# Forgetting attention and a bilinear feed-forward on one core: reciprocals for two query blocks at once, constants made by GpSimd, and a new order of all engines

## The chip, the cores and the metric

The kernel runs on one core of a Trainium2 chip. Its engines are TensorE (PE in the profile), VectorE (DVE), ScalarE (ACT), GpSimd (POOL) and SyncE (SP), which here only issues DMAs. Each engine takes its instructions in the order in which the program lists them, and waits on semaphores for what others make. The metric is the device time of one launch in microseconds. Three runs of the kernel before gave 401.5, 402.34 and 403.08 us.

## The reference

Eight batches of eight heads with 576 positions and 64 dimensions go through causal attention with forget gates; its output, as 4608 tokens of 512 values, goes through a feed-forward of width 1536 in which two projections are multiplied. Inputs and output are float32.

```python
scores = scale * np.matmul(q, k.transpose(0, 1, 3, 2))          # scale = 1/8
cum = np.cumsum(np.log(np.clip(f, 0.0001, 1.0)), axis=-1)
decay = cum[:, :, :, None] - cum[:, :, None, :]
scores = np.where(causal, -1000000000.0, scores + decay)
scores = scores - np.max(scores, axis=-1, keepdims=True)
attn = np.exp(scores)
attn = attn / (np.sum(attn, axis=-1, keepdims=True) + 1e-09)
x = np.matmul(attn, v).transpose(0, 2, 1, 3).reshape(B * S, H * D)
out = ((x @ w_a) * (x @ w_b)) @ w_out
```

## The kernel before

**Work.** A tile t stands for two heads of a batch, so there are 32 tiles; a unit is two tiles (four heads of a batch), 16 in all. A tile's 576 queries are five blocks: blocks 0 to 3 have 128 rows and block i has i + 1 key blocks up to the diagonal; block 4 has the last 64 rows of both heads, one above the other on the partitions. TensorE makes the scores of a unit in four groups of blocks (L401; `groups = [(1, 0), (2,), (3,), (4,)]`, taken in the turn 0, 1, 3, 2), with 32 rows of q and k at a time. Batches 0 to 2 add the decay with matmuls too and VectorE takes the row maxima (L488); for the others VectorE adds decay and takes the maximum in one instruction (L512). ScalarE takes the exponential and the row sum (L544, L550), one instruction for each head and block, except block 4, where one does both heads. VectorE takes the reciprocals of the sums (L557 for block 4, one column; L559 for the others, two columns, one for each head), and GpSimd multiplies the rows by them (L567, the norms). Tiles of probabilities are called PA (blocks 0 to 2) and PB (blocks 3 and 4); some lie in memory called spread or S. They are transposed, for batch 0 by TensorE into PSUM (psP, L591, copied out by VectorE or ScalarE), for the others by a DMA that SyncE issues (L583), into PTA, PTB and, early, xT. TensorE multiplies them by v (pv, L611, L613, L623 and, for block 4, L636), and ScalarE or VectorE copies the result to xT, the transposed tokens.

**Feed-forward.** For 256 to 512 tokens, TensorE makes psa and psb (L874) for each of twelve blocks of the width; psa is cast to a (L138 on ScalarE, L142 on VectorE), VectorE multiplies it by psb (L890), and TensorE makes the output pso (L899), which is copied to osb and stored (L914). The weights come by seven DMAs that GpSimd issues (L365) and that cast to 16 bits: 512 columns of wa and wb, then the other 1024 of each, then wout in three parts. The first psa and psb can run once batch 0 is through its attention and the first two loads are there.

**Start.** The forget gates f are clipped (L206), their logarithm is summed along the row (L213) and kept in a high and a low half (L142, L220) in 16 bits, which TensorE spreads over the rows (`rows`, L225). q and k are cast (L140, L142) and transposed in blocks of 32 by VectorE (L302). Constants (ones, a lower triangle `low`, `pick`, `eye`, `neg`, `sel`) come from the identity matrix.

**What sets the order.** All this is put into a list of numbered operations with what each depends on. A table written into the kernel, ORDER, lists the numbers in the order in which they are issued, for all engines together; a second, CHOICE, has a letter for each operation that more than one engine may do. The scheduler follows both as they stand (`tc.manual_schedule()`). Forty of the operations are fillers: four matmuls on the identity (L178, tile `idle`) with no use but to keep TensorE busy. PSUM has four banks for small tiles (tag ff: psa, psb, pso, pv, psP, idle, rows) and two double ones for scores (tag sc).

Of the kernel before, what the change touches and what calls it, by code (L numbers as in the profile page):

```python
# [14 lines left out]
MUL = mybir.AluOpType.mult  # L15
# [22 lines left out]
def kernel(  # L38
# [38 lines left out]
    def fixed(name, shape, dt=FP16):  # L77
        return perm.tile(shape, dt, tag=name, name=name)
# [5 lines left out]
    pick = fixed("pick", [128, 16])  # L84
    warm = fixed("warm", [128, 1], FP32)
# [62 lines left out]

    def lows(_):
        nc.vector.memset(low, 0.0)  # L150
        for a in range(1, 4):
            nc.vector.memset(low[:, a, 0:32 * a], 1.0)
        nc.vector.tensor_tensor_scan(out=step, data0=cw["1"][:, 0:32], data1=eye, initial=0.0, op0=MUL, op1=ADD)
        diag = spare[0][:, 1536:2176].rearrange("p (a x) -> p a x", x=160)[:, :, 0:32]
        nc.vector.tensor_scalar(out=diag, in0=step.unsqueeze(1).to_broadcast([128, 4, 32]), scalar1=-1.0, scalar2=1.0,
                                op0=MUL, op1=ADD)

    def picks(_):
        with nc.allow_low_precision("ones and zeros"):
            nc.vector.tensor_reduce(out=pick, in_=ident.rearrange("p (a r) -> p r a", r=16), axis=AXX, op=ADD)  # L160
            nc.vector.tensor_reduce(out=eye, in_=ident.rearrange("p (a n) -> p n a", n=32), axis=AXX, op=ADD)
        nc.vector.tensor_scalar(out=neg, in0=eye, scalar1=NEGBIG, scalar2=1.0, op0=MUL, op1=MUL)
        nc.vector.memset(sel, 0.0)
        for c in range(SETS):
            for e in range(2):
                nc.vector.tensor_copy(out=sel[:, c, e].rearrange("p (g e r) -> p g e r", e=2, r=16)[:, :, e],
                                      in_=eye[0:32, 16 * c:16 * c + 16].unsqueeze(1).to_broadcast([32, 4, 16]))
# [13 lines left out]
    o_pick = op("D", "pick", picks, [o_id])  # L181
# [15 lines left out]
    def f_ones(_):  # L197
        nc.vector.memset(warm, 1.0)
        nc.vector.memset(cw["1"], 1.0)
# [36 lines left out]
    o0 = op("D", "ones", f_ones)  # L236
# [3 lines left out]
    for lo, hi in ((0, 256), (256, S)):  # L240
# [7 lines left out]
        for n in range(SETS):  # L248
            bm = op("E", "crep", lambda _, n=n, a=a: rows_mm(n, *a), [o4, o5, o_pick], hi - lo)
# [5 lines left out]
    o_low = op("D", "low", lows, [o0, o_pick])  # L255
# [298 lines left out]
    def do_recip(t, i):  # L554
        st = T[("st", t)]
        if i == 4:
            nc.vector.reciprocal(out=st[:, 28:29], in_=st[:, 18:19])  # L557
        else:
            nc.vector.reciprocal(out=st[:, 20 + 2 * i:22 + 2 * i], in_=st[:, 10 + 2 * i:12 + 2 * i])  # L559
# [87 lines left out]

    last_row = [[] for _ in range(RING["bc"])]
# [16 lines left out]
    def softmax(t, g, qk, sc, rows, st_users, pu, norms):  # L665
# [4 lines left out]
        for i in groups[g]:  # L670
# [49 lines left out]
            rc = op("D", "rec", lambda _, i=i: do_recip(t, i), es)  # L720
            st_users[t].extend(es + [rc])
            for h in range(1 if i == 4 else 2):
                nm = op("P", f"norm{i}", lambda e, i=i, h=h: do_norm(e, t, i, h), [rc])
                st_users[t].append(nm)
                pu[kp].append(nm)
                norms.setdefault((t, part), []).append((i, nm))
# [252 lines left out]
    for t0, n in [(0, 256), (256, 256), (512, 256), (768, 384)] + [(1152 + 512 * n, 512 if n < 6 else 384) for n in range(7)]:  # L979
# [3 lines left out]
        42-44 0 20 41 2 1 64 26 31 23 54 55 45 16 32 13 12 71 46 37 47 56 18 67 27 65 34 72 73 68 48 24 19  # L983
# [3 lines left out]
        142 6 154 155 92 147 143 159 149 91 148 144 160 162 161 108 166-168 145 172 131 52 53 132 179 173 14  # L987
# [4 lines left out]
        310 305 1610 1612 246 214 247 158 226 215 227 311 234 189 1611 235 157 222 449 1614-1616 1613 283  # L992
        312 340 195 294 1617 223 1618 1620 228 229 341 1619 347 1621 236 342 450 94 343 191 232 288 1622 349
        260 237 233 1623 242 348 282 300 1624 366 211 344 1625 240 261 243 241 95 373 1626-1628 367 190 197
        1629 1630 1632 1631 196 302 1633 248 249 374 375 301 368 369 1634-1636 350 1638 284 262 263 392 1637
# [5 lines left out]
        1667 1670 455 1671-1673 1676 1677 421 388 382 381 389 456 1674 401 333 1678 357 413 1675 364 1679  # L1001
# [3 lines left out]
        465 460 500 409 463 505 1703 416 1704 480-482 424 508 440 428 422 1705 1706 509 471 477 483 479 510  # L1005
# [5 lines left out]
        1745-1747 1750 1748 548 1749 1752 1751 573 575 543 529 532 618 549 533 1753 1754 577 536 605 537 545  # L1011
        1755 1758 1759 1756 580 582 581 1713 550 552 606 553 1757 554-556 611 583 1760 544 578 585 1762 1763
# [7 lines left out]
        1817 1820 1818 683 690 694 798 704 662 1819 625 637 664-666 697 698 667 617 691 663 668 670 628 1821  # L1020
        1822 699 706 669 1825 716 1826 1827 700 1823 695 629 696 728 1830 1831 761 701 702 768 762 729 763
        1832 1835 1836 769-771 764 735 736 730 738 1824 703 765 1828 705 707 820 802 803 731 1833 799 800
# [113 lines left out]
```

## Time and profile before

| | us |
|---|---|
| median of 3 runs | 402.34 |
| profiled execution, span from the first to the last instruction | 400.7 |
| around the span, by the median | 1.6 |
| busy: TensorE, VectorE, GpSimd, ScalarE | 383.2, 315.3, 253.6, 250.0 |
| granted TensorE clock below full | from 17.2 to 24.0, and from 95.7 to 99.1 |

The busy time of an engine is the sum of its instructions' times. One with a share near 100% sets the time wherever it is full; idle time of the others costs nothing there. The view by stretches gives busy times between two moments, and the granted clock of TensorE as a mean (0.5 is half speed throughout). The view of waits names what ended an engine's idle time; the chain that ended last is followed back from the last instruction.

### The profile page before, as it was taken

What the parts mean: (1) busy time and instruction counts of PE and PEld (TensorE: products, weight loads), DVE (VectorE), ACT (ScalarE), POOL (GpSimd) and SP (SyncE); (2) the same over time, 40 slices, a digit from 0 to 9 for tenths busy, and PEclk for the clock granted to TensorE, in tenths of its full rate; (3) what the DMA queues carried; (4) which work ended last, traced back from release to release, by engine and by line L of the source; (5) the groups of instructions that cost most, each with busy time, mean ns of one, the idle gap of its engine ahead of it and who ended that gap; (6) DMA issues with size and microseconds to landing.
All of it is one profiled execution on the core that took longest, in us unless ns stands there. A gap on an engine that the chain in (4) does not pass through costs nothing.

```text
span 400.7 us, 11076 instructions
## 1 busy us (share of the span) xinstructions
PE 383.2 (96%) x4040; PEld 212.0 (53%) x4040; DVE 315.3 (79%) x907; ACT 250.0 (62%) x757; POOL 253.6 (63%) x424
## 2 busy tenths in 40 slices
PE   8598799998999999999999999999999999999996
PEld 7466576765855544454445454544444444444553
DVE  8989798976778988997988889898969892373560
ACT  5798766666667778758785777577868673300011
POOL 3889876887397876897896849787968553000000
PEclk9889999998999999999999999999999999999999
DMA  7999989989999999999999999999997729000102
GB/s 282 240 186 289 204 177 224 213 150 215 208 301 208 227 171 330 201 277 212 295 187 286 211 255 273 233 241 190 276 187 218 157 66 202 28 2 36 71 0 79
DMA packets 148311, 78.22 MB, mean 195 GB/s; under 512 B 130592, under 2 KB 133408, under 8 KB 148256
## 3 DMA queue, kind: packets, MB, share of 16 engines
q1 hardware_dynamic: 144272, 72.53, 77.4%
q0 software_dynamic: 3696, 4.72, 7.0%
q8 instruction: 31, 0.51, 0.5%
q10 hardware_dynamic: 288, 0.26, 0.2%
q14 instruction: 24, 0.20, 0.1%
HBM read 49.69 MB, written 9.58 MB: 148 GB/s over the span
## 4 chain that ended last, share of the span: by engine, by line
PE 79%; DMA 9%; DVE 4%; POOL 2%; ACT 2%; issue 2%; SPq 0%; POOLq 0%; DVEq 0%; ACTq 0%
PE pso L899 22%; PE psa L874 22%; PE psb L874 21%; PE sc L401 8%; DMA wa<-in_moe_w_a_dram 5%; PE pv L611 2%; DVE st L488 2%; DMA k<-in_k_dram 1%; PE pv L613 1%; PE sc L636 1%; DMA PTB<-spread 1%; DMA PTB<-PB 1%; DVE qT L302 1%; PE pv L623 1%; ACT PB L550 1%
## 5 line engine op out<-in xcount | busy, mean ns | idle before, releaser
L874 PE MATMUL psa<-xT,wa 128*128 128x512 f16 (+2 forms) x528 | 116.2, 343 | 2.3 <-DMA wa<-in_moe_w_a_dram 1.7
L874 PE MATMUL psb<-xT,wb 128*128 128x512 f16 (+2 forms) x528 | 116.2, 343 | 0.1
L899 PE MATMUL pso<-wout,ht 128*128 128x512 f16 (+1 forms) x444 | 98.4, 374 | 0.0
L567 POOL TENSOR_SCALAR PA<-PA,st 128x128 f16<-128x128 f16 (+2 forms) x162 | 76.0, 482 | 31.8 <-DVE st L559 20.4
L890 DVE TENSOR_TENSOR ht<-psb,a 128x512 f16<-128x512 f32 (+2 forms) x132 | 76.2, 589 | 22.0 <-PE psb L874 15.0
L512 DVE CUSTOM_DVE_ANT_0 S<-sc,spread 128x128 f32<-128x128 f32 (+3 forms) x160 | 86.7, 567 | 7.7 <-PE sc L401 5.4
L138 ACT CAST a<-psa 128x512 f16<-128x512 f32 (+2 forms) x85 | 43.5, 515 | 55.9 <-PE psa L874 53.8
L874 PEld LDWEIGHTS <-wa 128*128 128x128 f16 x528 | 50.1, 99 | 45.5 <-issue 3.7
L874 PEld LDWEIGHTS <-wb 128*128 128x128 f16 x528 | 50.4, 99 | 41.5 <-issue 1.7
L567 POOL TENSOR_SCALAR PB<-PB,st 128x512 f16<-128x512 f16 (+1 forms) x84 | 58.7, 712 | 15.7 <-DVE st L559 14.6
L550 ACT ACTIVATE PA<-S,st 128x256 f16<-128x256 f32 (+2 forms) x120 | 59.9, 502 | 12.5 <-DVE st L512 12.4
L899 PEld LDWEIGHTS <-ht 128*128 128x128 f16 x444 | 41.7, 98 | 46.8 <-issue 1.3
L488 DVE TENSOR_REDUCE st<-sc 128x2 f32<-128x512 f32 (+7 forms) x68 | 46.3, 723 | 6.0 <-PE sc L401 5.3
L401 PE MATMUL sc<-kT,qT 32*128 32x128 f16 (+5 forms) x960 | 41.7, 272 | 5.5 <-ACT PA L550 2.1
L550 ACT ACTIVATE PB<-S,st 128x512 f16<-128x512 f32 x40 | 28.5, 714 | 7.9 <-DVE st L512 7.9
L401 PEld LDWEIGHTS <-qT 32*128 32x128 f16 (+1 forms) x960 | 18.6, 96 | 26.7 <-issue 14.4
L142 DVE CAST a<-psa 128x512 f16<-128x512 f32 (+2 forms) x47 | 26.2, 560 | 7.2 <-PE psa L874 6.6
L559 DVE RECIPROCAL st<-st 128x2 f32<-128x2 f32 x128 | 18.5, 157 | 14.0 <-ACT PA L550 8.7
L142 POOL CAST k<-k 128x1152 f16<-128x1152 f32 (+1 forms) x15 | 20.5, 1367 | 8.9 <-DMA k<-in_k_dram 8.9
L138 ACT COPY osb<-pso 128x512 f32<-128x512 f32 (+1 forms) x22 | 12.4, 570 | 19.9 <-PE pso L899 15.1
L138 ACT CAST xT<-pv 128x512 f16<-128x512 f32 (+2 forms) x39 | 17.0, 446 | 11.8 <-PE pv L636 5.8
L140 POOL TENSOR_SCALAR q<-q 128x1152 f16<-128x1152 f32 (+1 forms) x15 | 20.6, 1372 | 5.0 <-DMA q<-in_q_dram 4.2
(98 smaller groups left out, 491.5 us busy)
## 6 DMA issues: line engine op xcount, KB each, us to landing
spread<-cum_d SPq DMA_DIRECT2D x20, 576.0 KB, 5.9
out_dram<-osb SPq DMA_DIRECT2D x35, 256.0 KB, 3.8
q<-in_q_dram SPq DMA_DIRECT2D x15, 576.0 KB, 7.3
k<-in_k_dram SPq DMA_DIRECT2D x15, 576.0 KB, 5.2
v<-in_v_dram SPq DMA_DIRECT2D x32, 256.0 KB, 6.1
wout<-in_moe_w_out_dram POOLq DMA_DIRECT2D x3, 512.0 KB, 8.7
v<-in_v_dram SPq DMA_DIRECT2D x8, 128.0 KB, 7.2
wb<-in_moe_w_b_dram POOLq DMA_DIRECT2D x1, 1024.0 KB, 13.5
```

The source lines that it names most:

```text
L138: nc.scalar.copy(out=out_, in_=in_)
L140: ENG[e].tensor_scalar(out=out_, in0=in_, scalar1=0.125, scalar2=1.0, op0=MUL, op1=MUL)
L142: ENG[e].tensor_copy(out=out_, in_=in_)
L401: nc.tensor.matmul(out=dst, lhsT=lhsT, rhs=rhs, start=start, stop=stop, skip_group_check=True)
L488: nc.vector.tensor_reduce(out=m if i == 4 else st[:, 2 * i:2 * i + 2][:, h:h + 1] if isinstance(x, list) else m, in_=y, axis=AXX, op=MAX, ...
L512: nc.vector.tensor_tensor_reduce(out=o, in0=x, in1=y, scale=-1.0, scalar=3e38, op0=ADD, op1=MIN, accum_out=m)
L550: nc.scalar.activation(out=p_blocks(t, i)[:, :, h, :], in_=x.rearrange("p (j k) -> p j k", k=128), func=EXP, scale=sign, bias=st[:, c:c + ...
L559: nc.vector.reciprocal(out=st[:, 20 + 2 * i:22 + 2 * i], in_=st[:, 10 + 2 * i:12 + 2 * i])
L567: ENG[e].tensor_scalar(out=p, in0=p, scalar1=st[:, c:c + 1], scalar2=1.0, op0=MUL, op1=MUL)
L874: nc.tensor.matmul(out=o, lhsT=w16[:, db, 128 * fb:128 * fb + 128], rhs=tokens(db, t0, n), start=(db == 0), stop=(db == 3))
L890: nc.vector.tensor_tensor(out=ht[:, 0:n], in0=T.pop(("psb", t0, fb))[:, 0:n], in1=T.pop(("a16", t0, fb))[:, 0:n], op=MUL)
L899: nc.tensor.matmul(out=o, lhsT=T[("ht", t0, fb)][:, 128 * tb:128 * tb + 128], rhs=wout16[:, fb, c], start=(fb == 0), stop=(fb == 11))
```

## The change

Three things change. First, a reciprocal instruction now serves two query blocks where a tile's sums for them stand beside each other: blocks 1 and 0 (four columns, as they are one group of scores already), and blocks 3 and 4 (three columns). Block 2 keeps its own. So each tile has three such instructions, not five, 96 instead of 160 in all, and the norms of blocks 3 and 4 (1 and 0) both wait for the row sums of both. Second, the constants are made by GpSimd; `pick` and `eye` by halving sums of the identity instead of reductions, in operations of their own (`pick`, `sel`, `lowm`, `ones`). The scan that makes `step`, and the diagonal blocks of `low`, stay on VectorE. Third, ORDER and CHOICE are new. TensorE does the same matmuls as before, fillers included, in another order. VectorE does two instructions fewer of the early kind (a cast of q with 512 columns, and the 320-column half of the subtraction at L220, now both on GpSimd) and makes fewer copies of transposed blocks (3 instead of 7, the others on ScalarE). The last two stores go through SyncE's queue instead of ScalarE's.

```diff
-    def do_recip(t, i):
+    def do_recip(t, lo, hi):
         st = T[("st", t)]
-        if i == 4:
-            nc.vector.reciprocal(out=st[:, 28:29], in_=st[:, 18:19])
-        else:
-            nc.vector.reciprocal(out=st[:, 20 + 2 * i:22 + 2 * i], in_=st[:, 10 + 2 * i:12 + 2 * i])
+        nc.vector.reciprocal(out=st[:, lo + 10:hi + 10], in_=st[:, lo:hi])
...
-            rc = op("D", "rec", lambda _, i=i: do_recip(t, i), es)
+            sums = summed.setdefault((t, g if g < 2 else 2), [])
+            sums.append((i, es))
+            if len(sums) < (2 if g != 1 else 1):
+                continue
+            cols = [c for j, _ in sums for c in ((18,) if j == 4 else (10 + 2 * j, 11 + 2 * j))]
+            es = [x for _, xs in sums for x in xs]
+            rc = op("D", "rec", lambda _, lo=min(cols), hi=max(cols) + 1: do_recip(t, lo, hi), es)
...
+    def low_blocks(_):
+        nc.gpsimd.memset(low, 0.0)
+        for a in range(1, 4):
+            nc.gpsimd.memset(low[:, a, 0:32 * a], 1.0)
+
     def lows(_):
-        nc.vector.memset(low, 0.0)
-        for a in range(1, 4):
-            nc.vector.memset(low[:, a, 0:32 * a], 1.0)
         nc.vector.tensor_tensor_scan(out=step, ...)
...
     def picks(_):
-            nc.vector.tensor_reduce(out=pick, in_=ident.rearrange("p (a r) -> p r a", r=16), axis=AXX, op=ADD)
-            nc.vector.tensor_reduce(out=eye, in_=ident.rearrange("p (a n) -> p n a", n=32), axis=AXX, op=ADD)
-        nc.vector.tensor_scalar(out=neg, in0=eye, scalar1=NEGBIG, scalar2=1.0, op0=MUL, op1=MUL)
-        nc.vector.memset(sel, 0.0)
+        nc.gpsimd.tensor_tensor(out=half, in0=ident[:, 0:64], in1=ident[:, 64:128], op=ADD)
+        nc.gpsimd.tensor_tensor(out=eye, in0=half[:, 0:32], in1=half[:, 32:64], op=ADD)
+        nc.gpsimd.tensor_tensor(out=pick, in0=eye[:, 0:16], in1=eye[:, 16:32], op=ADD)
+        nc.gpsimd.tensor_scalar(out=neg, in0=eye, scalar1=NEGBIG, scalar2=1.0, op0=MUL, op1=MUL)
+
+    def selections(_):
+        nc.gpsimd.memset(sel, 0.0)
...
     ORDER = """
-        42-44 0 20 41 2 1 64 26 31 23 54 55 45 16 32 13 12 71 46 37 47 56 18 67 27 65 34 72 73 68 48 24 19
+        0 42 27 24 40 3 44 45 38 46 39 11 7 33 4 1 2 47 48 14 56 18 49-52 69 73 77 57-59 26 17 81 70 71 67
```

GpSimd's queue ahead of the weights, first of before. The rows are its instructions from the first value cast on (nv), with the norms of the first tiles (PA and spread) and the loads of weights (wa, wb):

```order
22 L142 CAST nv_73<-v_355 128x1024
23 L567 TENSOR_SCALAR PA<-PA,st 128x128 x2
24 L567 TENSOR_SCALAR PA<-PA,st 128x2x128 x2
25 L365 DMA wa_70<-in_moe_w_a_dram 128x4x512
26 L567 TENSOR_SCALAR PA<-PA,st 128x2x128 x2
27 L365 DMA wb_71<-in_moe_w_b_dram 128x4x512
28 L567 TENSOR_SCALAR PA<-PA,st 128x128
29 L142 CAST nv_74<-v_377 128x1024
30 L567 TENSOR_SCALAR spread_80<-spread_80,st 128x2x128
31 L365 DMA wb_71<-in_moe_w_b_dram 128x4x1024
32 L365 DMA wa_70<-in_moe_w_a_dram 128x4x1024
```

In the changed kernel the first load of wb stands at number 27 of the queue, ahead of all norms. These are the rows of the other three loads:

```order
45 L571 TENSOR_SCALAR spread_80<-spread_80,st 128x128
46 L372 DMA wa_71<-in_moe_w_a_dram 128x4x512
47 L571 TENSOR_SCALAR PA<-PA,st 128x128
48 L571 TENSOR_SCALAR spread_81<-spread_81,st 128x2x128 x2
49 L571 TENSOR_SCALAR spread_81<-spread_81,st 128x128
50 L571 TENSOR_SCALAR spread_80<-spread_80,st 128x2x128
51 L372 DMA wa_71<-in_moe_w_a_dram 128x4x1024
52 L571 TENSOR_SCALAR spread_80<-spread_80,st 128x128
53 L571 TENSOR_SCALAR spread_80<-spread_80,st 128x2x128
54 L141 TENSOR_SCALAR q_675<-q_572 128x1152
55 L143 CAST k_677<-k_378 128x1152
56 L372 DMA wb_72<-in_moe_w_b_dram 128x4x1024
```

The first load of wa moved behind nine norms and two value casts (numbers 36 to 45; four norms and one value cast were ahead of it before), the large load of wa behind more norms, and that of wb behind these and the whole casts of q and k for batch 1's second half; before, the two large loads followed each other.

TensorE near the end of batch 1's attention, before. The scores of the last group but one (sc_2204) are followed by the value products for block 4 of a tile whose transpose comes from spread (L636), then by those for its other blocks (L623):

```order
2699 L401 LDWEIGHTS xT_66
2700 L401 MATMUL sc_2204<-neg,xT_66 128x32
2701 L636 LDWEIGHTS nv_74
2702 L636 MATMUL pv_2237<-PTB,nv_74 64x64
2703 L636 LDWEIGHTS nv_74
```

The changed kernel has the block 4 of an earlier tile behind the same scores (sc_2167), whose transpose was issued well before, then projections, and only then the first products that read a transpose from spread (2822 and, for block 4, 2874):

```order
2708 L408 MATMUL sc_2167<-neg,xT_67 128x32
2709 L640 LDWEIGHTS nv_75
2710 L640 MATMUL pv_2197<-PTB,nv_75 64x64
...
2815 L886 LDWEIGHTS wa_71
2816 L886 MATMUL psa<-xT_70,wa_71 128x256
2817 L627 LDWEIGHTS nv_75
2818 L627 MATMUL pv<-xT_70,nv_75 64x128
...
2822 L627 MATMUL pv<-PTB,nv_75 64x128
...
2874 L640 MATMUL pv_2342<-PTB,nv_75 64x64
```

Between 2729 and 2816 stand eleven groups of four matmuls for psa and psb (128x256), which stood behind the value products before.

More of the change, by code (lines that the diff above doesn't have):

```diff
@@ L84 @@
     pick = fixed("pick", [128, 16])
+    half = fixed("half", [128, 64])
     warm = fixed("warm", [128, 1], FP32)
@@ L158, in picks @@
     def picks(_):
-        with nc.allow_low_precision("ones and zeros"):
-            nc.vector.tensor_reduce(out=pick, in_=ident.rearrange("p (a r) -> p r a", r=16), axis=AXX, op=ADD)
-            nc.vector.tensor_reduce(out=eye, in_=ident.rearrange("p (a n) -> p n a", n=32), axis=AXX, op=ADD)
-        nc.vector.tensor_scalar(out=neg, in0=eye, scalar1=NEGBIG, scalar2=1.0, op0=MUL, op1=MUL)
-        nc.vector.memset(sel, 0.0)
+        nc.gpsimd.tensor_tensor(out=half, in0=ident[:, 0:64], in1=ident[:, 64:128], op=ADD)
[4 more added lines that the diff above has]
+        nc.gpsimd.memset(sel, 0.0)
         for c in range(SETS):
             for e in range(2):
-                nc.vector.tensor_copy(out=sel[:, c, e].rearrange("p (g e r) -> p g e r", e=2, r=16)[:, :, e],
+                nc.gpsimd.tensor_copy(out=sel[:, c, e].rearrange("p (g e r) -> p g e r", e=2, r=16)[:, :, e],
                                       in_=eye[0:32, 16 * c:16 * c + 16].unsqueeze(1).to_broadcast([32, 4, 16]))
@@ L180 @@
     o_id = op("P", "const", constants)
-    o_pick = op("D", "pick", picks, [o_id])
+    o_pick = op("P", "pick", picks, [o_id])
+    o_sel = op("P", "sel", selections, [o_pick])
+    o_lowm = op("P", "lowm", low_blocks)
     for _ in range(40):
@@ L197, in f_ones @@
     def f_ones(_):
-        nc.vector.memset(warm, 1.0)
-        nc.vector.memset(cw["1"], 1.0)
+        nc.gpsimd.memset(warm, 1.0)
+        nc.gpsimd.memset(cw["1"], 1.0)
     def warm_table(func):
@@ L235 @@
     s_users = [take(o_f, "S") for _ in range(2)]
-    o0 = op("D", "ones", f_ones)
+    o0 = op("P", "ones", f_ones)
     o0.after.append(o_f)
@@ L646, in do_ev4 @@
         cast(e, xT[pr][:, b, SF:S], T.pop(("pv4", t)))
+    summed = {}
     last_row = [[] for _ in range(RING["bc"])]
@@ L719, in softmax @@
                 es.append(ex)
-            rc = op("D", "rec", lambda _, i=i: do_recip(t, i), es)
-            st_users[t].extend(es + [rc])
[L722 to L726, printed above, removed]
+            sums = summed.setdefault((t, g if g < 2 else 2), [])
[5 more added lines that the diff above has]
+            rc = op("D", "rec", lambda _, lo=min(cols), hi=max(cols) + 1: do_recip(t, lo, hi), es)
+            st_users[t].extend(es + [rc])
+            for j in [j for j, _ in sums]:
+                for h in range(1 if j == 4 else 2):
+                    nm = op("P", f"norm{j}", lambda e, j=j, h=h: do_norm(e, t, j, h), [rc])
+                    st_users[t].append(nm)
+                    pu[kp].append(nm)
+                    norms.setdefault((t, part), []).append((j, nm))
     def attention(u):
@@ new lines @@
+        175 176 131 43 129 238 172 173 55 239 270 267 271 218 219 260 261 94 89 184 246 247 185 37 186 191
+        268 192 22 1536 1537 1540 1541 1538 193 1542 197 148 149 187 189 190 1539 1543 161 163 154 156 194
+        196 15 204 205 198 199 177 178 180 179 181 183 284 285 1544-1546 1548 1549 188 274 162 288 182 277
+        286 155 150 195 296 96 297-299 301 300 289 1550 1547 1551 167 168 290 214 215 287 95 216 217 1552
+        1554 228 229 200 230 231 201 240 241 212 213 330 337 339 338 1553 1555-1557 1560 331 1558 1559 97
@@ new lines @@
+        489 409 446 355 318 414 417 418 453 1646 403 389 488 354 1652 424 404 1653 1656 444 1650 1654 445
+        1658 473 499 1655 474 1657 1660-1662 1664 1663 1666 1665 448 1659 475 476 1668 500 1669 1672 388 463
+        1670 1671 501 395 393 425 1667 470 428 429 462 387 416 419 421 422 420 1674 502 510 430 1673 1676
+        548 549 551 469 1675 1678 522 525 1677 1680-1682 1679 1683 464 447 1684 1686 1685 1687 461 1688 1689
+        431 506 1690 523 526 524 1692 1693 1696 490 487 495 496 508 550 1694 1695 477 479 1698 478 527 1697
```

84 lines of the change are left out of this document (44 added, 40 removed), and 116 rows, old and new, of the table ORDER.

## The prediction

> **What bounds the kernel now.** I read the page's first part, then the table of busy time by stretches, then TensorE's waits, the chain that ended last, and last the timeline at the places that these name. The first rows are busy time and share of the span by engine:
>
> ```profile
> PE 383.2 (96%) x4040; PEld 212.0 (53%) x4040; DVE 315.3 (79%) x907; ACT 250.0 (62%) x757; POOL 253.6 (63%) x424
> ```
>
> TensorE is busy for 383.2 of 400.7 us, so 17.5 us is all that better order could win at a full clock. The table by stretches (length; then busy time of PE, PEld, DVE, ACT and POOL; granted clock; DMA share; GB/s) says where it lies:
>
> ```profile
> 0.00:10.00 10.00, 8.02 (x82) 7.19 (x83) 8.21 (x25) 5.82 (x10) 3.62 (x10) 1.00 0.79 283
> 10.00:20.00 10.00, 5.28 (x138) 4.01 (x136) 9.62 (x23) 7.67 (x32) 8.86 (x20) 0.86 0.99 240
> 20.00:30.00 10.00, 9.05 (x153) 6.52 (x154) 8.92 (x22) 9.16 (x33) 8.16 (x16) 0.80 1.12 187
> 40.00:50.00 10.00, 7.75 (x134) 6.06 (x136) 7.95 (x21) 7.32 (x30) 8.40 (x12) 1.00 1.13 204
> 70.00:80.00 10.00, 9.16 (x183) 7.46 (x176) 9.53 (x21) 6.59 (x22) 8.13 (x14) 1.00 1.27 213
> 90.00:100.00 10.00, 8.22 (x100) 5.42 (x100) 6.13 (x13) 6.31 (x18) 7.10 (x13) 0.83 1.07 213
> 110.00:200.00 90.00, 90.00 (x886) 45.29 (x885) 78.81 (x253) 65.86 (x197) 72.95 (x122) 1.00 1.03 247
> 200.00:300.00 100.00, 99.95 (x902) 46.57 (x899) 86.17 (x288) 71.94 (x217) 77.30 (x127) 1.00 1.00 234
> 300.00:390.00 90.00, 90.00 (x609) 43.73 (x602) 57.13 (x143) 33.19 (x86) 23.72 (x44) 1.00 0.36 88
> 390.00:400.70 10.70, 7.37 (x46) 4.28 (x44) 0.60 (x2) 1.54 (x3) 0.00 (x0) 0.94 0.21 74
> ```
>
> From 110 to 390 us TensorE has 0.05 us of idle time: there it is the bound, and the work of VectorE and GpSimd lies beside it. The idle time is in the first 110 us (17.5 less 3.33 at the end and 0.05, so 14.1 us), and three stretches of it have a clock under 1. TensorE's waits, as total, number and longest, name what ended the gaps:
>
> ```profile
> PE sc L401 <- ACT PA L550: 2.1, 1, 2.1
> PE sc L401 <- DVE st L559: 2.1, 1, 2.1
> PE pv L636 <- DMA PTB<-spread: 1.8, 1, 1.8
> PE psa L874 <- DMA wa<-in_moe_w_a_dram: 1.7, 1, 1.7
> ```
>
> Each comes once. The first two lie before 20 us, the third at 94 us, the fourth at 44 us. So the question is what the change does to four places; a saving elsewhere is worth nothing while TensorE stays full.
>
> **The constants.** Before, VectorE makes them from 0.81 us until it clips the forget gates at 3.76 us:
>
> ```profile
> 0.81 0.06 DVE L198 MEMSET warm<- 128x1 f32 x1 [0.81 <-PEq L1120]
> 3.76 0.51 DVE L206 TENSOR_SCALAR cum_f<-cum_f 64x320 f32<-64x320 f32 x2
> cum_f<-in_f_dram SPq DMA_DIRECT2D x1, 144.0 KB, 2.7
> ```
>
> The gates (last row: KB, us from issue to landing) come by a DMA of 2.7 us, so most of these three microseconds lie beside that wait: I count 0.3 us for the removal. GpSimd then does the same work before the first cast of q:
>
> ```profile
> 1.01 0.29 POOL masks.py:199 TENSOR_SCALAR_AFFINE_SELECT ident<-ident 128x128 f16<-128x128 f16 x1
> 5.54 0.86 POOL L140 TENSOR_SCALAR q<-q 128x640 f16<-128x640 f32 x1 [4.23 <-DMA q<-in_q_dram]
> 11.05 0.99 POOL L173 MEMSET nv<- 64x512 f16 x2
> ```
>
> It is idle for 4.23 us there. By its own 0.50 us for a 512-wide memset and 0.29 us for a pass over the identity, the fifteen or so instructions make an estimated 3 to 4.2 us; the cover holds, just. Without it the cast of q and all behind it would come late by the excess. The Trainium skill ("GPSIMD Engine Reference", 4.1 Engine selection) advises against two-input elementwise work on GpSimd, calling it about twice as slow as VectorE. The subtraction that both engines do here weighs against the factor:
>
> ```profile
> 7.52 1.03 DVE L220 TENSOR_TENSOR wout<-cum_f,wout 32x320 f16<-32x320 f32 x1
> 8.18 0.91 POOL L220 TENSOR_TENSOR wout<-cum_f,wout 32x256 f16<-32x256 f32 x1
> ```
>
> That is 3.2 ns a column on VectorE and 3.6 on GpSimd. By the page's factor the constants would pass 5.54 us by a little and the gain below would shrink by that; by the row it stays.
>
> **The start, to 30 us.** The chain that ended last runs through VectorE there (start, length):
>
> ```profile
> 8.48 1.20 DVE qT L302
> 12.72 1.10 DVE q L140
> ```
>
> The new order gives the 320-column half of the subtraction (1.03 us) and the last early cast of q (1.10 us) to GpSimd, which the table has busy for 3.62 and 8.86 us of the first two stretches of 10, and puts one reciprocal of 0.15 us in place of two. With the 0.3 us of the clip VectorE's chain loses 2.6 us; GpSimd is nearly full then and takes some of it back. I take 1.9 us, between nothing (GpSimd takes the chain over) and 2.6.
>
> **The weights.** Part of that stops at the next wait. The weights come through GpSimd's DMA queue:
>
> ```profile
> 17.05 0.98 POOL L365 DMA_DIRECT2D wa<-in_moe_w_a_dram  x1
> 21.71 0.81 POOL L365 DMA_DIRECT2D wb<-in_moe_w_b_dram  x1
> 22.51 21.65 DMA wa<-in_moe_w_a_dram
> 44.21 0.61 PE L874 MATMUL psa<-xT,wa 128*128 128x256 f16 x4 [1.65 <-DMA wa<-in_moe_w_a_dram]
> ```
>
> Four loads (3 MB) go from 17.05 to 44.16 us: 0.11 MB a microsecond beside all other transfers. The new order issues one half megabyte early, near 10 us (an estimate from the queue's rows, as the next ones), then the other behind five more norms and a second value cast, at an estimated 20.9 us, and the large loads near 24 and 29 us. The 2.5 MB from 20.9 us end by that rate near 43.5 us. Also, the first product that needs the last load (now wb, not wa) stands behind 25 transposes and one score group. Between 0 and 2 us of the start's gain survive; I take **1.2**, since landing and need both come out near 43.4 us.
>
> **The merged reciprocals.** VectorE's rows by group (busy us, mean ns, idle before), and the two-column reciprocals alone in the first 110 us:
>
> ```profile
> L559 DVE RECIPROCAL st<-st 128x2 f32<-128x2 f32 x128 | 18.5, 157 | 14.0 <-ACT PA L550 8.7 <-ACT PB L550 4.9
> L557 DVE RECIPROCAL st<-st 128x1 f32<-128x1 f32 x32 | 4.7, 153 | 0.0
> L142 DVE COPY xT<-psP 128x768 f16<-128x768 f16 x7 | 3.7, 546 | 0.0
> 0.00:110.00 110.00, 5.97 (x44) 0.95 1.03 217
> ```
>
> One column more costs 4 ns, so 160 instructions become 96 of about 0.16 us and some 8 us of VectorE's time go. Of the 128 with two columns only 44 come before 110 us, a third; behind it TensorE hides the rest. A third of 8 us is 2.7 us, and four copies of transposed blocks (0.55 us each) go to ScalarE: 4.9 us. But from 50 to 90 us TensorE idles for 0.84 us, in the stretch from 70 to 80, and what VectorE holds back before 44 us is counted above: I take **0.5 us**, from 0 to 2. The price is that a norm waits for both blocks. The later block's exps are two of this kind, the norm behind them is on GpSimd:
>
> ```profile
> L550 ACT ACTIVATE PB<-S,st 128x512 f16<-128x512 f32 x40 | 28.5, 714 | 7.9 <-DVE st L512 7.9
> POOL PB L567 <- DVE st L559: 14.6, 15, 3.3
> ```
>
> So the norm of the earlier block starts up to 1.4 us later, the pair's last norm does not, or by less than that norm's own 0.75 us. GpSimd is 63% busy, and no wait of TensorE for PTB<-PB is in the list. I cost it at 0, with up to 0.75 us for each of the twelve units from batch 2 on.
>
> **The gap at 94 us.** This is the largest term. Rows of TensorE's timeline and the clock:
>
> ```profile
> 92.25 0.26 PE L401 MATMUL sc<-neg,xT 32*128 32x32 f16 x16
> 94.28 0.35 PE L636 MATMUL pv<-PTB,nv 128*64 128x64 f16 x10 [1.77 <-DMA PTB<-spread]
> 95.70:99.10 3.40, 3.40 (x19) 2.42 (x17) 1.01 (x3) 2.77 (x9) 1.36 (x2) 0.50 0.93 199
> ```
>
> TensorE waits 1.77 us for a transposed tile, and 1.4 us later its clock is halved for 3.4 us, in which full work takes 1.7 us longer. In the new order the value products on these two tiles stand behind eleven projections of four matmuls each. In the stretch of the last row 19 matmuls, nearly all of this kind, took 3.4 us at half the clock, so 44 take about 4 us at the full one, and that work lies between the scores and the products. The wait goes, and with it the half clock: **3.5 us**. The bounds are 0 (the tile comes 4 us later too) and 3.5. The Trainium skill ("TensorE: Matmul & The Clock Gate", HAM oscillation) sets the limit for an idle gap at about 3.4 us. By that, a gap of 1.77 us would not cost a half clock and the term would be 1.8; the row's 0.50 behind such a gap is the measurement that decides.
>
> **The end.** The last store moves from ScalarE's queue to SyncE's:
>
> ```profile
> 397.59 0.37 ACT L138 COPY osb<-pso 128x256 f32<-128x256 f32 x1 [2.22 <-DMA out_dram<-osb]
> ```
>
> The copy starts 0.2 us after the last matmul (394.80 + 2.56), held by ScalarE's own DMA issue. I count 0, between −0.3 and +0.5 us.
>
> **Sum.** 1.2 + 0.5 + 3.5 = 5.2 us, so a span of 395.5 us. The median is 402.34 us, 1.64 above the profiled span; with that, **397.1 us**, 1.3% less. What a measurement of this kernel can tell from no change is about 0.5%, or 2 us.
>
> **Rivals.** *No change* (chance 0.18): the 8 us of lighter VectorE lie beside a full TensorE, the start's gain ends in the weights, and the gap at 94 us comes back at another late tile: 0 to 2 us less, about 401.5. For it speaks that only four waits carry anything; against it that the new order puts 4 us of ready work into the largest. *Slower by the weights* (0.12): one mechanism, at 40 to 50 us. The last large load, issued 6.5 us later than before's last (29 against 22.51), may take the 21.65 us that one took, for the other transfers of the start go on beside it: it lands at 50.7 us instead of 44.16. TensorE, out of work near 43.4, then goes on 6.5 us later than before, and behind such a wait I expect a halved clock as at 94 us (1.7 us): 402.3 + 6.5 + 1.7 − 4.0 for the other two terms = 406.5. For it speaks that the issue stands behind norms and two casts; against it that only 1 MB is left to load by then. It decides from a landing behind 48.5 us on. *Slower by the merged norms* (0.05): where a transposed tile has no slack, each later norm pushes TensorE; twelve units at up to 0.75 us make 9 us, less 5.2: 406. *More than forecast* (0.07): the 2.6 us at the start also take away the half clock from 17.2 to 24 us,
>
> ```profile
> 17.20:24.00 6.80, 5.68 (x82) 4.03 (x85) 5.64 (x16) 6.11 (x28) 6.57 (x12) 0.50 1.01 212
> ```
>
> in which 5.68 us of work would need half as long: 2.8 us more, 394.3.
>
> **How the numbers follow.** The forecast has 0.58, with its own range of 395 to 400. Faster by over 0.5% is 0.58 + 0.07, same 0.18, slower 0.17. The range from 393.0 to 404.0 takes in the forecast, no change, and what is more than forecast, with about a microsecond for the spread of the runs (401.5 to 403.08); it leaves out the two slower cases.
>
> **What would show it.** Right: no wait for PTB<-spread and a clock of 1.00 from 90 to 100 us; the first psa 1.9 us earlier; the wait for wb or wa under 2 us; reciprocals 96, some 15 us. Wrong: a landing of the last 1024 KB load behind 45 us, a clock below 1 behind 30 us, GpSimd's first cast of q behind 5.6 us, or waits for PTB<-PB in TensorE's list.

## The result, and the profile after

The changed kernel is slower. Its median is 407.25 us over four runs (405.88 to 407.83), against 402.13 us for the kernel before on the same chips; the ratio is 1.0132, with a 95% interval of 1.0104 to 1.0159. The forecast was 397.1 us. The profiled execution is the slowest of the four (407.83 us, span 406.1).

The page's first part and the stretches of the changed kernel, with the columns of before:

```profile
span 406.1 us, 10966 instructions
PE 385.0 (95%) x4040; PEld 212.3 (52%) x4040; DVE 304.9 (75%) x830; ACT 250.7 (62%) x754; POOL 259.0 (64%) x441
0.00:10.00 10.00, 7.25 (x79) 6.26 (x80) 6.18 (x10) 5.63 (x9) 8.50 (x25) 1.00 0.79 271
90.00:100.00 10.00, 8.70 (x143) 6.87 (x143) 6.22 (x11) 7.29 (x22) 8.98 (x16) 1.00 1.06 187
110.00:200.00 90.00, 89.06 (x850) 44.15 (x848) 77.23 (x236) 64.22 (x193) 72.83 (x118) 1.00 1.02 251
200.00:300.00 100.00, 97.66 (x849) 44.84 (x848) 85.83 (x270) 68.14 (x208) 73.84 (x123) 0.98 0.91 226
300.00:390.00 90.00, 89.16 (x631) 42.77 (x630) 47.85 (x125) 38.73 (x99) 27.28 (x49) 1.00 0.41 98
390.00:406.00 16.00, 12.88 (x80) 7.53 (x77) 5.38 (x10) 1.92 (x4) 0.00 (x0) 1.00 0.13 50
```

VectorE is 10.4 us lighter, as the change meant. TensorE, full from 110 to 390 us before (0.05 us idle), now idles there for 0.94 + 2.34 + 0.84 = 4.1 us, and the 0.98 in the stretch from 200 to 300 us is 3.4 us at half clock, from 230.6 us on, or 1.7 us of work. Over the whole span idle time grew by 3.6 us (17.5 to 21.1) and busy time by 1.8, with the same 4040 recorded matmuls and, while TensorE worked, half clocks of the same length in both (6.8 us before 30 us and 3.4 later); what makes the busy time longer is not shown. Its waits behind 110 us (there was none to list before):

```profile
PE sc L408 <- DVE st L519: 2.8, 3, 1.0
PE pv L640 <- DMA PTB<-PB: 0.6, 1, 0.6
```

Scores of a unit wait for VectorE's decays (L519) of the group before to free the double bank of PSUM. The timeline from 218 to 234 us shows why VectorE is late; first the rows of SyncE and VectorE, then TensorE's, and last a stretch with its clock:

```profile
218.88 0.36 SPq L926 DMA_DIRECT2D out_dram<-osb  x1
219.34 0.37 SPq L295 DMA_DIRECT2D q<-in_q_dram  x1
219.77 0.45 SPq L926 DMA_DIRECT2D out_dram<-osb  x1
219.77 6.92 DMA out_dram<-osb
226.78 0.69 DVE L143 COPY osb<-pso 128x512 f32<-128x512 f32 x1 [1.66 <-DMA out_dram<-osb]
227.38 0.68 DVE L519 CUSTOM_DVE_ANT_0 S<-sc,spread 128x512 f32<-128x512 f32 x1
228.74 0.23 PE L408 MATMUL sc<-kT,qT 32*128 32x128 f16 x2 [0.91 <-DVE st L519]
229.96 0.51 PE L408 MATMUL sc<-kT,qT 32*128 32x128 f16 x22 [0.99 <-DVE st L519]
230.60:234.10 3.50, 3.50 (x10) 1.24 (x9) 3.42 (x14) 2.74 (x11) 3.50 (x6) 0.51 0.76 169
```

There are two osb buffers. A store issued at 219.77 us beside loads of q and v lands 6.92 us later (the median of the 35 is 2.8). VectorE's copy of the output of two copies later has to wait for it, and the four decays stand behind that copy in VectorE's queue. TensorE waits twice, and 0.7 us after the second wait its clock is at half (last row). The same stands at 173 to 185 us, where a store lands after 7.8 us and TensorE waits 0.89 us; no half clock follows there. The waits of copies for stores, from 110 to 400 us:

```profile
DVE osb L143 <- DMA out_dram<-osb: 3.1, 2, 1.7
ACT osb L139 <- DMA out_dram<-osb: 3.8, 2, 2.1
```

VectorE's line was not there before; ScalarE's was 3.1 us, 2.2 of it for the last copy of all, which falls behind 400 us now. Slow stores are not new: the slowest took 8.3 us in the kernel before and 7.8 now.

At the start, the constants fill GpSimd until 6.5 us, and its casts come behind them:

```profile
1.25 0.53 POOL L151 MEMSET xT<- 128x512 f16 x1
4.55 1.95 POOL L171 COPY xT<-eye 32x64 f16<-32x64 f16 x4
6.48 0.66 POOL L227 TENSOR_TENSOR wout<-cum_f,wout 32x256 f16<-32x256 f32 x1
7.98 0.86 POOL L141 TENSOR_SCALAR q<-q 128x640 f16<-128x640 f32 x1
31.40 0.60 PE L886 MATMUL psa<-xT,wa 128*128 128x256 f16 x4
```

The first cast of q starts at 7.98 instead of 5.54 us (that of k, which now goes first, at 7.09 instead of 7.28), and the first psa at 31.40 instead of 30.37 us.

### The profile page after: what moved, and what is told of

The parts are those of the page before. It is cut to its first block, busy times and chain, and to the rows that moved or that the text cites. A ratio compares the mean times of both kernels' runs of the same rounds, so it can differ in the third digit from the quotient of the medians.

```text
span 406.1 us, 10966 instructions
## 1 busy us (share of the span) xinstructions
PE 385.0 (95%) x4040; PEld 212.3 (52%) x4040; DVE 304.9 (75%) x830; ACT 250.7 (62%) x754; POOL 259.0 (64%) x441
## 4 chain that ended last, share of the span: by engine, by line
PE 49%; DVE 15%; DMA 11%; POOL 9%; ACT 8%; issue 6%; SPq 1%; DVEq 0%; ACTq 0%; POOLq 0%
PE psb L886 15%; PE psa L886 15%; PE pso L911 9%; DMA out_dram<-osb 6%; PE sc L408 5%; DVE S L519 5%; DVE st L495 3%; ACT PA L557 3%; POOL PA L571 2%; POOL spread L571 2%; DMA PTB<-PB 2%; ACT PB L557 2%; DVE ht L902 2%; DMA PTB<-spread 1%; POOL nv L143 1%
## 5 line engine op out<-in xcount | busy, mean ns | idle before, releaser
L902 DVE TENSOR_TENSOR ht<-psb,a 128x512 f16<-128x512 f32 (+2 forms) x132 | 75.1, 586 | 24.2 <-PE psb L886 17.0
L519 DVE CUSTOM_DVE_ANT_0 S<-sc,spread 128x128 f32<-128x128 f32 (+3 forms) x160 | 86.3, 568 | 8.5 <-PE sc L408 3.6
L408 PEld LDWEIGHTS <-qT 32*128 32x128 f16 (+1 forms) x960 | 19.1, 96 | 29.1 <-issue 15.2
L143 DVE CAST a<-psa 128x256 f16<-128x256 f32 (+2 forms) x49 | 26.3, 538 | 10.0 <-PE psa L886 9.8
L139 ACT COPY osb<-pso 128x512 f32<-128x512 f32 (+1 forms) x24 | 13.7, 573 | 27.1 <-PE pso L911 21.0
L557 ACT ACTIVATE PA<-sc,st 128x256 f16<-128x256 f32 (+2 forms) x42 | 19.5, 481 | 10.9 <-DVE st L495 10.9
L571 POOL TENSOR_SCALAR spread<-spread,st 128x128 f16<-128x128 f16 (+4 forms) x36 | 19.9, 559 | 6.4 <-DVE st L563 6.1
L563 DVE RECIPROCAL st<-st 128x4 f32<-128x4 f32 (+2 forms) x96 | 15.2, 164 | 10.3 <-ACT PA L557 5.2
```

The source lines that it names most:

```text
L139: nc.scalar.copy(out=out_, in_=in_)
L143: ENG[e].tensor_copy(out=out_, in_=in_)
L408: nc.tensor.matmul(out=dst, lhsT=lhsT, rhs=rhs, start=start, stop=stop, skip_group_check=True)
L519: nc.vector.tensor_tensor_reduce(out=o, in0=x, in1=y, scale=-1.0, scalar=3e38, op0=ADD, op1=MIN, accum_out=m)
L557: nc.scalar.activation(out=p_blocks(t, i)[:, :, h, :], in_=x.rearrange("p (j k) -> p j k", k=128), func=EXP, scale=sign, bias=st[:, c:c + ...
L563: nc.vector.reciprocal(out=st[:, lo + 10:hi + 10], in_=st[:, lo:hi])
```

## The experiments

Three theories went into them. Theory 1: the new order makes copies wait for stores, and the rest follows. Theory 2: the merged reciprocals hold up norms and transposes. Theory 3: the constants cost on GpSimd. Each ratio is against the kernel before on the same chip. Where a diff below only tells of places in ORDER, nothing else was changed.

**The parts alone.** e1 has only the merged reciprocals, e2 only the constants, in the old order; e3 has only the new order:

```diff
# e1, on before: the merged do_recip and its caller, as in the change; ORDER is the old one without 64 reciprocals, with norms moved behind the merged ones
# e2, on before; low, ones, pick, eye and neg likewise, as in the change
-        nc.vector.memset(sel, 0.0)
+        nc.gpsimd.memset(sel, 0.0)
...
# e3, on after: constants on nc.vector again, and
+        for x, y in {(10, 14): ((12, 14), (10, 12)), (14, 16): ((14, 16),), (16, 19): ((18, 19), (16, 18))}[lo, hi]:
+            nc.vector.reciprocal(out=st[:, x + 10:y + 10], in_=st[:, x:y])
```

> The order and the constants of before, with the reciprocals merged; norms that stood ahead of the merged reciprocal move behind it, and nothing else. Theory 1 (the loss comes from copies of pso on VectorE that wait for slow stores, which is the new order's): as before, 401 to 403 us. Theory 2 (the merged reciprocals hold the norms and transposes): 404 to 407 us. Theory 3 (the constants on GpSimd): as before.

> The order and the reciprocals of before, with the constants made by GpSimd. Theory 3 (GpSimd needs 5.2 us for them, its first cast of q begins at 8 instead of 5.5 us, and what that delays lasts to the end): 404 to 407 us. Theory 1 and theory 2: 401.5 to 403.5 us, for the delay is taken up at the wait for the weights at 44 us.

> The new order, but constants on VectorE and each block's reciprocal by itself, at the place of the merged one. Theory 1: about as slow as the changed kernel, 405 to 408 us. Theory 2 and theory 3 both lose nothing here that the order alone would not lose: 400 to 403 us if the order itself is good. The norms still wait for both blocks here, so theory 2 in its form that the wait costs, not the instruction, would also give 405 to 408; e1 tells these apart.

e1 took 409.47 us (1.0180, 1.0131 to 1.0229; two of its six runs near 405.7, the others from 408.1 to 411.3), more than any theory gave; e2 400.63 (0.9977, 0.9959 to 0.9995), a little under before; e3 405.62 (1.0100, 1.0075 to 1.0126). So the new order by itself carries some 4 us of the loss, the constants in the old order carry none, and merging in the old order carries about 7. Theory 2 holds there, which says nothing yet of the new order.

**Where merging costs.** e7 merges from tile 8 on only, e15 as e7 but blocks 1 and 0 alone:

```diff
+            if t < NP * EARLY:                # e15: or i >= 3
+                rc = op("D", "rec", ...)      # one block's columns, as before
```

> The order and constants of before, with the reciprocals merged from tile 8 (batch 2) on only; norms that stood ahead of the merged reciprocal move behind it. Theory 2 (where nothing else is reordered, the merged reciprocal makes norms and then transposes late, and TensorE waits for PTB): 403.5 to 406.5 us, with waits for PTB<-PB behind 110 us. Rival (the loss of the kernel with all merged came from batch 0's transposes in the first 45 us alone): 401 to 403 us.

> As e7 (old order and constants, merged from tile 8 on), but only blocks 1 and 0 share a reciprocal, blocks 3 and 4 keep their own. If e7's loss comes from the norms of PB and so from PTB: 401.5 to 403 us, and no waits for PTB<-PB. If it comes from PA as well: 403.5 to 405.5 us.

e7 took 406.14 us (1.0091, 1.0056 to 1.0126), e15 401.96 (0.9995, 0.9968 to 1.0023). The waits of TensorE behind 110 us in e7:

```profile
PE sc L633 <- DMA PTB<-PB: 4.1, 4, 1.1
```

In e15's list that line is absent. So it is the pair of blocks 3 and 4. GpSimd's waits for the reciprocals of PB from 110 to 400 us, in the kernel before, in e7 and in e15:

```profile
POOL PB L567 <- DVE st L559: 6.5, 10, 1.5
POOL PB L564 <- DVE st L556: 12.2, 13, 2.5
POOL PB L564 <- DVE st L556: 3.4, 6, 0.9
```

Block 4's norm, early in the old order, waits for block 3, GpSimd's queue waits with it, and the transposed tile PTB comes up to 1.1 us late for products that stand ready. Blocks 1 and 0 cost nothing. The rest of e1's loss, about 3 us by subtraction, would then come with the first eight tiles: in e1's trace TensorE waits 2.2 us at 40 us for a norm of PB, and its clock is 0.79 from 30 to 46 us, against 1.00 in the kernel before.

**Stores.** e4 moves the two copies that waited behind the four decays; e5 gives osb a third buffer:

```diff
# e4, on after: in ORDER 1829 (copy) goes behind 861 (the last decay), with its store; 1897 behind 1051
# e5, on after
-    RING = {..., "ht": 15, "a16": 3, "osb": 2, "ff": 4}
+    RING = {..., "ht": 13, "a16": 3, "osb": 3, "ff": 4}
```

> The changed kernel with two of VectorE's copies of pso to osb (those that wait at 181 and at 227 us for a store) moved behind the four decay instructions that stand behind them. Theory 1: TensorE's stalls of 1.1 us at 184 us and of 2 us at 227 us go, and with the second the half clock of 3.4 us behind it: 402.5 to 405 us. Theory 2 and 3: no change, 406.5 to 408 us.

> The changed kernel with three buffers for osb instead of two (and 13 for ht instead of 15, to make room; never more than 13 of these are in use in this order). Theory 1 (a copy of pso waits for the store of two copies before, and VectorE's and ScalarE's other work behind it): the waits of the copies for out_dram, 6.9 us on VectorE and ScalarE, go, and TensorE's stalls at 184 and 228 us with them: 402 to 405.5 us. If the stalls come from something else that is late there: 406.5 to 408.5 us.

e4 took 411.69 us (1.0252, 1.0223 to 1.0282): the opposite of what theory 1 said. The timeline of SyncE and TensorE in e4 says why:

```profile
181.21 5.45 SPq L926 DMA_DIRECT2D out_dram<-osb  x2
186.76 1.46 SPq L587 DMA_TRANSPOSE PTA<-PA  x1
188.32 0.52 SPq L295 DMA_DIRECT2D q<-in_q_dram  x1
188.90 5.95 SPq L587 DMA_TRANSPOSE PTB<-PB  x2
195.47 0.25 PE L640 MATMUL sc<-PTB,nv 128*64 128x64 f16 x4 [1.63 <-DMA PTB<-PB]
```

The store of the moved copy went along in the list, but no other instruction of SyncE stood between its old and new place, so it kept its place in SyncE's queue and now waited there for the copy (185.61 us, 180.96 in the changed kernel), with the transposes behind it; PTB came late, and TensorE waited 1.63 us for that. TensorE's wait for the decays at 184 us did go. The experiment moved the wait to another queue, and its time does not test theory 1. e5 does, for it moves nothing in ORDER: 404.44 us (1.0066, 1.0044 to 1.0089). No copy waits for out_dram any more, and TensorE's line shrinks from 2.8 to

```profile
PE sc L408 <- DVE st L519: 1.1, 2, 0.9
```

So the stores cost 2.8 us of the 5.1. In the traces idle time from 110 to 390 us falls from 4.1 to 2.3 us and the half clock at 231 us is gone. The control e11, the kernel before with the third buffer:

> The kernel before with three buffers for osb and 13 for ht, a control. Theory 1 (the waits for stores are the new order's): no difference, 401.5 to 403 us. If a third buffer helps any order: 399 to 401 us.

It took 402.36 us (1.0028, 1.0000 to 1.0057): no gain there. The cost of these waits is the new order's.

**Constants in the new order.** e6 has all of them on VectorE, e14 only sel, e9 joins e6 and e5:

```diff
# e14, on after
     def selections(_):
-        nc.gpsimd.memset(sel, 0.0)
+        nc.vector.memset(sel, 0.0)
...
-                nc.gpsimd.tensor_copy(out=sel[:, c, e]...
+                nc.vector.tensor_copy(out=sel[:, c, e]...
```

> The changed kernel with the constants made by VectorE again, at the same places of the order. Theory 3 (GpSimd's chain of constants delays the first casts by 2 us, in this order): 404.5 to 406.5 us, the lead of 1 to 2 us from 20 to 100 us on. Rival (the delay is taken up at the weights, as when they moved alone): 406.5 to 408 us.

> The changed kernel with one of the constants, sel (a memset and four copies, 2.5 us on GpSimd at 3.9 to 6.5 us), on VectorE. If the length of GpSimd's chain ahead of its first casts is what the constants cost: 405 to 406.3 us, as with all of them on VectorE, and the first cast of k on GpSimd near 5 us. If it is not the length: 406.5 to 408 us.

> The changed kernel with three buffers for osb (13 for ht) and the constants on VectorE. If stores and constants are two separate causes, their effects add: 2.8 and 1.6 us off the changed kernel's 407.3, so 402.5 to 403.5 us. If both come to the same place, as e5 alone: 404 to 405 us.

e6 took 405.60 us (1.0092, 1.0065 to 1.0119), e14 405.27 (1.0074, 1.0045 to 1.0104), e9 403.64 (1.0035, 1.0012 to 1.0059). By the medians all constants cost 1.6 us in the new order, and sel alone accounts for it within the intervals. That is at the edge of what the runs can tell: e6's interval overlaps the changed kernel's (1.0104 to 1.0159), e14's just touches it. How is open. In e14 GpSimd's chain ends at 3.9 us, but its first cast of k starts at 6.72 us, not near 5 as I had expected, since the subtraction (L227) that the new order put ahead of it waits for VectorE:

```profile
5.59 1.17 POOL L227 TENSOR_TENSOR wout<-cum_f,wout 32x256 f16<-32x256 f32 x1 [1.71 <-DVE wout L143]
6.72 0.85 POOL L143 CAST k<-k 128x512 f16<-128x512 f32 x1
```

That is 0.4 us less than the changed kernel's 7.09, less than the gain. In e6 the first cast of q comes later than in the changed kernel (8.70 us, for it waits for its DMA), and so does the first psa (32.76 us). Nor does TensorE idle less behind 110 us; e6, then e14:

```profile
110.00:390.00 280.00, 275.59 (x2344) 132.05 (x2335) 211.89 (x629) 171.38 (x500) 174.38 (x290) 1.00 0.78 194
110.00:390.00 280.00, 275.10 (x2336) 132.14 (x2334) 211.23 (x629) 171.49 (x500) 172.75 (x287) 1.00 0.77 192
```

That is 4.4 and 4.9 us against 4.1. What both traces lack is the half clock at 231 us, 1.7 us of work. With one trace of each this is a rival, not a finding: the constants may matter only by moving two waits apart. It would fit e9, which is 0.8 us below e5, where 1.6 was expected and where that half clock is gone already; these two intervals overlap as well.

**Merging in the new order.** e10, e13 and e16 put single reciprocals into e9. In e10 each stands directly behind its exps and norms are moved ahead too; in e13 reciprocals stand some 8 operations behind the exps from tile 8 on and close norms move along; in e16 no norm moves:

```diff
# on e9, in ORDER: rec of a block from behind both blocks' exps to behind its own
+            if t >= NP * EARLY:               # e10: for all tiles
+                rc = op("D", "rec", ...)
```

> As e9, but each block's reciprocal by itself and directly behind its own exps, and the norms of the block that is ready first directly behind that. Theory 2 (the merged reciprocal costs in the new order too, as in the old one): 400 to 402 us, faster than e9 by 1 to 2. Rival (the new order was made for the merged ones, and waits for them nowhere): as e9, within 0.7 us, or slower by the 64 instructions.

> As e9, but from tile 8 on each block has its own reciprocal, which stands some 8 operations (in the order of all engines) behind its last exp, as the median of the old order has it, and not directly behind it as in e10; norms move only where they followed the merged reciprocal closely. Theory 2 (the merged reciprocals cost in the new order too): 400.5 to 402.5 us. Rival (the new order has room for them): as e9, 403 to 404.5 us.

> As e13, but no norm moves in GpSimd's queue: only the reciprocals are single again from tile 8 on and stand some 8 operations behind their last exps. A norm that waited for its merged reciprocal can start earlier, and nothing stands in another place on GpSimd, SyncE and TensorE. Theory 2 (waiting for the merged reciprocal costs in the new order): 401 to 402.8 us, with fewer waits of GpSimd for the reciprocal. Rival (it costs nothing there): as e9, 403 to 404.5 us, and then e13's 17 us came from the norms' places in GpSimd's queue.

e10 took 533.85 us (1.3285), e13 420.28 (1.0431, 1.0384 to 1.0477), e16 405.62 (1.0079, 1.0042 to 1.0116). The first two show only how hard an engine's queue punishes a place: in e13 GpSimd reaches norms whose reciprocals are not there, with casts of k and other tiles' norms behind them, and TensorE waits

```profile
PE sc L640 <- DMA PTB<-PB: 10.4, 5, 5.9
```

e16 was meant as the test. Its median is 2 us above e9's, in intervals that overlap, so this split gains nothing. But it did not free the norms: GpSimd waits longer for reciprocals from 110 to 400 us, not less; the first two rows are e9's, the others e16's:

```profile
POOL PA L571 <- DVE st L563: 10.9, 8, 2.5
POOL PB L571 <- DVE st L563: 8.4, 10, 1.8
POOL PA L571 <- DVE st L563: 14.6, 9, 3.9
POOL PB L571 <- DVE st L563: 9.7, 9, 2.1
```

So whether waiting for both blocks costs something in the new order stays open. e3 and e6, which differ only in whether the merged place has one instruction or two, have 405.62 and 405.60 us: the instructions that were saved are worth nothing that these runs can tell.

**Both orders in one.** e8 has the new order up to 142 us, with the constants on VectorE, and the old order and single reciprocals behind, e12 the old order with the constants on GpSimd and a third osb buffer:

> The new order up to the first scores of unit 7 (about 142 us), merged reciprocals for the tiles before it, constants on VectorE; behind that the old order and single reciprocals. Theory 1 in its wide form (the new order gains 2 us and more in the first 110 us, and all of the loss arises behind 140 us): 396.5 to 399.5 us, faster than both. Rival (the gain of the first part is given back wherever the work behind it meets full engines): 401 to 404 us.

> The kernel before with the constants on GpSimd (as in e2) and three buffers for osb. As e2 by theory 1: 400 to 402 us, a little under before. A version that beats both kernels clearly would be under 400.

e8 took 402.72 us (1.0006, 0.9979 to 1.0034), e12 401.10 (0.9976, 0.9953 to 0.9998). That e8 is back at the time of before fits a loss that lies wholly behind 142 us, but the lead of the first part, hoped for as 2 us and more, did not reach the end. The best of all runs is the old order with the constants on GpSimd (e2, e12), 0.23% under before, which both intervals only just tell from nothing.

## Why the prediction was wrong, by its own steps

- **The constants.** "An estimated 3 to 4.2 us; the cover holds, just". It held in the old order, where the first cast of q starts at 5.54 us as before (e2), and failed in the new one, where the constants took 1.25 to 6.50 us, 5.25. What the estimate left out is what runs beside them. The four copies for sel, first in e2 with VectorE idle, then in the changed kernel beside VectorE's work on the gates:

```profile
3.78 0.75 POOL L167 COPY xT<-eye 32x64 f16<-32x64 f16 x4
4.55 1.95 POOL L171 COPY xT<-eye 32x64 f16<-32x64 f16 x4
```

The row that weighed against a factor of two was misread in the same way. VectorE's subtraction of 1.03 us ran beside GpSimd's cast of k (7.28 to 8.20 us). In e7, where GpSimd is idle then, it takes 0.48 us, 1.5 ns a column; GpSimd's takes 0.66 us in e7, 2.6 ns. The factor is 1.7, not 1.1.

```profile
7.44 0.48 DVE L220 TENSOR_TENSOR wout<-cum_f,wout 32x320 f16<-32x320 f32 x1
9.35 0.66 POOL L220 TENSOR_TENSOR wout<-cum_f,wout 32x256 f16<-32x256 f32 x1
```

In time the constants cost nothing in the old order (e2), and some 1.6 us, at the edge of the noise, in the new one (e6).
- **The start.** Forecast 1.9 us earlier at the first psa; measured 1.0 us later, in one execution each. I took VectorE's chain to be shortened by what leaves it and let GpSimd take back 0.7 us. More than that was taken back, below the lower end that the text named ("GpSimd takes the chain over"). By what is not shown: in e6, where GpSimd makes no constants, the first psa comes later still, at 32.76 us. From 0 to 90 us TensorE's idle time is the same in both profiles to 0.1 us (11.9).
- **The weights.** The mechanism was right: both large loads land by 42.6 us, no wait of TensorE for wa or wb is left, and the rival of late weights, my main slower case (0.12), did not come. The 1.2 us did not arrive: the start brought no lead, and TensorE's idle time before 90 us is the same in all, so other waits took the place of this one.
- **The reciprocals.** 96 and 15.2 us, as forecast, worth nothing that can be told, and not 0.5 us (e3 against e6). The rival of the norms (0.05) is right for the old order, where blocks 3 and 4 cost 4 us (e7, e15), and open for this one, since e16 did not free them.
- **The gap at 94 us.** Forecast 3.5 us. The clock is 1.00 from 90 to 100 us now, but a wait for the same tiles stands at 98 us, 1.3 us instead of 1.8:

```profile
PE pv L627 <- DMA PTB<-spread: 1.3, 1, 1.3
```

The two transposes were issued later as well (from 90.06 us before, at 92.05 and 93.92 now), which the text had as the term's lower bound. Idle time and half clock from 90 to 110 us fell from 1.78 + 0.45 + 1.7 to 1.30 + 0.58, a gain of 2 us. The direction was right, the term mis-sized.
- **From 110 to 390 us.** This is the step that failed and made the sign: "there it is the bound, and the work of VectorE and GpSimd lies beside it", a term of 0. It held for the old order only. A full TensorE was a property of that order, in which no late copy and no late decay reached TensorE, and not of the work. The new order has 4.1 us of idle time and 1.7 us of half clock there. The one rival that spoke of this stretch, the merged norms, named another cause. Of the 5.1 us of loss, waits for stores are 2.8 (e5) and the constants perhaps 0.8 to 1.6 more (e9, e6, both at the edge of the noise); about 1.4 stay open (e9's 1.0035). In e9 TensorE still waits 1.1 us for decays at 244 us, where stores play no part.
- **The end.** Forecast 0; 3.1 us of idle time behind 390 us instead of 3.3.

Of the four signs of being wrong three came: a first cast of q behind 5.6 us (7.98), a clock below 1 behind 30 us (at 230.6) and PTB<-PB in TensorE's list (0.6 us). None of the four looked for a copy that waits for a store, which was the largest cause found.

## What to carry to other kernels

A stretch in which an engine is full is full for one order; when all orders are made anew, cost the stretch by the waits that the new order can bring, and look first at what stands ahead of a releasing instruction in its queue: here a copy that needs a buffer back from a DMA. Look at the slowest landing, not the median (7.8 us against 2.8 here), before you settle for two such buffers; whether a third helps depends on the order (e5 against e11). Price a move between VectorE and GpSimd from rows in which the other one is idle, then ask what will run beside them, and before merging two instructions, see which of their users was early.

## What the runs showed of the hardware

VectorE's instructions got longer while GpSimd worked, and GpSimd's beside VectorE's (the copies for sel above). In the kernel before, `step` and the diagonal of `low` take 0.16 and 0.20 us at 3.5 us, where GpSimd is idle (it waits for q until 5.54). In the changed kernel they run beside casts on GpSimd; first two rows of before, then three of the changed kernel:

```profile
3.46 0.16 DVE L153 TENSOR_TENSOR_SCAN step<-cum_f,eye 128x32 f16<-128x32 f16 x1
3.65 0.20 DVE L155 TENSOR_SCALAR xT<-step 128x128 f16<-128x128 f16 x1
7.25 0.73 DVE L156 TENSOR_TENSOR_SCAN step<-cum_f,eye 128x32 f16<-128x32 f16 x1
8.01 0.89 DVE L158 TENSOR_SCALAR xT<-step 128x128 f16<-128x128 f16 x1
7.09 0.80 POOL L143 CAST k<-k 128x512 f16<-128x512 f32 x1
```

They end at 7.98 and 8.90 us, within 0.1 us of the ends of the casts of k (7.89) and q (7.98 + 0.86). In e6, where GpSimd waits for q from 7.4 to 8.7 us, the second takes 0.20 us again:

```profile
6.72 0.73 DVE L156 TENSOR_TENSOR_SCAN step<-cum_f,eye 128x32 f16<-128x32 f16 x1
7.48 0.20 DVE L158 TENSOR_SCALAR xT<-step 128x128 f16<-128x128 f16 x1
8.70 0.86 POOL L141 TENSOR_SCALAR q<-q 128x640 f16<-128x640 f32 x1 [1.34 <-DMA q<-in_q_dram]
```

The Trainium skill ("SBUF — State Buffer", Terms) says that the two engines share a pair of ports which one holds for a whole instruction while the other blocks. The rows agree: some 0.6 us for each of these two. So moving small work from VectorE to GpSimd can also lengthen what stays.

The length of a single wait does not say whether TensorE's clock falls. In the changed kernel it was at half for 3.4 us from 230.6 us on, behind waits of 0.91 and 0.99 us that ended at 228.74 and 229.96 us. In e3 a single wait of 1.50 us that ended at 183.78 us was followed by 0.50 from 184.5 to 187.9 us, and in the kernel before one of 1.77 us was. But one of 1.65 us (before, ending at 44.21 us) was not, nor one of 1.36 us (e6, ending at 186.50 us).
